# Two more head pairs of a windowed-attention kernel in the packed, split-operand form

## Chip, cores and metric

The kernel runs on one core of a Trainium2 chip. The metric is the device time of one execution in microseconds (us), lower is better. The three runs shown before the change have a median of 701.85 us (701.72 to 701.91).

## What is computed

Attention over a sliding window with a few sink keys, for 4 batches of 8 heads, 768 tokens and head size 64; then, on the 3072 rows of 512 numbers that the heads give together, a two-layer network with a leaky ReLU. All of it is float32, with the accuracy of float32.

```
scores = scale * q @ k.T
keep   = (pos[None, :] < n_sink) | ((rel >= 0) & (rel < window))   # n_sink = 4, window = 128
a      = softmax(where(keep, scores, -1e9))
x      = (a @ v).transpose(0, 2, 1, 3).reshape(B * S, H * D)
h      = x @ w_in                       # 512 -> 2048
out    = maximum(0.01 * h, h) @ w_out   # 2048 -> 512
```

## The kernel before

The work is cut into eight **units**: half a batch each, 384 tokens in T = 3 blocks of 128, even units the first half, odd ones the second. A unit has four **pairs** of heads. `attention_stream` does the attention of unit after unit, pair after pair, in small steps; `mlp_stream` does the two-layer network in 16 steps per unit (`fc` = 0 to 15, a slice of 128 of the 2048 hidden columns each). While the network works on unit u, the attention of unit u + 1 runs between its matmuls. TensorE's order is written out by this interleaving (TensorE is the one engine in `MANUAL`); the order on the other engines is the scheduler's, and each of them takes its instructions strictly in that order.

A step of the network: 12 matmuls into the bank `h` (line 554: three products of split operands for each of four column groups), then `g`: ScalarE's 0.01 h (564), VectorE's maximum (571), ScalarE's rounded copy `gh` (572), GpSimd's rest `gl` (573); and 9 matmuls of the second layer for the step before (591). In unit 0 every step writes the same bank `h`, so the matmuls of a step wait for VectorE's `g` of the step before.

Only while the network works on unit 0 are the weights made ready, two steps ahead: each step loads two slices (`wiraw`, `woraw`, line 173), VectorE turns the 64-bit numbers into float32 with three instructions for each slice (185, 187, 189), ScalarE rounds them (198) and GpSimd takes the rest (199). The raw slices go into the tag `raw` of `iopool`, which has three buffers.

A pair of heads has two forms, chosen by `native(u)`: units 0 and 1 are native, all others packed.

- **Native** (`attend`, first branch): one load `qkn` for two heads. For each block j two float32 matmuls with 64 rows each (299), a softmax of 260 columns for each head (311 on VectorE, 313 on ScalarE), and four float32 transposes (340) that ScalarE copies out (345). The sums go through two small VectorE instructions (323, 324), a broadcast on GpSimd (327) and transposes on TensorE (375, 378); VectorE applies them after the product with the values (407).
- **Packed** (second branch): one load `qkraw` for each head, with the operands twice. ScalarE rounds them (264) and GpSimd takes the two rests (265, 267): `split_head`. For each block two rounded matmuls with 128 rows (304); VectorE folds the 260 columns to 132 with a predicated copy (490) and a softmax over 132 (311). After three blocks VectorE scales the probabilities itself (497, 498, 499). `turn_packed` has three transposes (351) and, on VectorE, two masked products out of them (370), for the second head also the sink columns (356). `values` has one matmul for all sinks (391); VectorE takes the rest `xl` (412), and `split_sinks` another (257).

Packed heads load into the same tag `raw` as the weights, all but the first head of unit 2. `late_masks` builds the masks of the packed form in unit 1, pair 1.

Of the kernel before, what the change touches and what calls it, by code (L numbers as in the profile page):

```python
# [9 lines left out]
F32 = mybir.dt.float32  # L10
# [10 lines left out]
P = 128  # L21
B, H, S, D = 4, 8, 768, 64
DM, DF = 512, 2048
NB = S // P
NPAIR = H // 2
# [4 lines left out]
TU = T * P  # L30
NSK = 4
SKR = P
# [6 lines left out]
SCALE = 1.0 / D ** 0.5  # L39
MASKED = 1.0e38  # L40
DEEP = 9.0e8
NATU = 2
LEAD = 10
LEAD0 = 3
LAGT = 2
LAGG = 3
LAGV = 4
LAGP = 5
# [99 lines left out]
def fast_path(ctx, tc, cpool, qp, qk, vu, vs, vt, wq, out, ident, lims, wz, negm, wmin, wmax):  # L148
# [3 lines left out]
    xpool = ctx.enter_context(tc.tile_pool(name="xpool", bufs=2))  # L152
# [11 lines left out]
    raws, vraws, svs = {}, {}, {}  # L164
# [49 lines left out]

    def native(u):
        return u < NATU

    def load_pair(u, pair):  # L220
        b, half = divmod(u, 2)
        n = TU + NK[half]
        raw = apool.tile([P, TU + NK[1]], F32, tag="qksp", name=f"qkn{u}_{pair}")
        nc.sync.dma_start(out=raw[:, 0:n], in_=qp[half][pair])
        raws[u, pair] = raw

    def load_values(u, pair):
        b, half = divmod(u, 2)
        vr = apool.tile([P, 4 * P], F32, tag="v", name=f"v{u}_{pair}")
        nc.sync.dma_start(out=vr[:, 0:NVB[half] * P], in_=vu[half][b, pair])  # L230
        vraws[u, pair] = vr

    def load_head(u, h):
        b, half = divmod(u, 2)
        n = TU + NK[half]
        if native(u - 1) and h == 0:
            raw = apool.tile([P, TU + NK[1]], F32, tag="qksp", name=f"qkraw{u}_{h}")
        else:
            raw = iopool.tile([P, TU + NK[1]], F32, tag="raw", name=f"qkraw{u}_{h}", bufs=3)
        nc.sync.dma_start(out=raw[:, 0:n], in_=qk[half][b, h])  # L240
        raws[u, h] = raw

    def load_sinks(u, pair):
        if native(u):
            sv = apool.tile([SKR, TU], F32, tag="sv", name=f"sv{u}_{pair}")
            nc.sync.dma_start(out=sv[0:SKN, :], in_=vs[u // 2, pair])
            svs[u, pair] = sv
            return
        raw = xpool.tile([SKR, TU], F32, tag="rb", name=f"svr{u}_{pair}", bufs=1)[:, 0:P]
        nc.sync.dma_start(out=raw, in_=vt[u // 2, pair])  # L250
        svs[u, pair] = raw

# [30 lines left out]
    def score_bank(u, name):  # L283
        tags = ("s0", "s1", "o0", "o1") if u == 0 else ("s0", "s1")
        seq["s"] += 1
        return bank(tags[(seq["s"] - 1) % len(tags)], name)
# [6 lines left out]
    def scores(u, pair, j, heads, sp):  # L293
        k0, kn = KSL[u % 2][j]
        pss = [score_bank(u, f"s{u}_{2 * pair + o}_{j}") for o in heads]
        if native(u):
            for o, ps in zip(heads, pss):
                rows = slice(o * D, (o + 1) * D)
                nc.tensor.matmul(ps[:, 0:kn], lhsT=sp[rows, j * P:(j + 1) * P],  # L299
                                 rhs=sp[rows, TU + k0:TU + k0 + kn], start=True, stop=True)  # L300
        else:
            n = NK[u % 2]
            for c, off in enumerate((0, TU + n)):
                nc.tensor.matmul(pss[0][:, 0:kn], lhsT=sp[:, off + j * P:off + (j + 1) * P],  # L304
                                 rhs=sp[:, TU + k0:TU + k0 + kn], start=c == 0, stop=c == 1)
        return pss
# [8 lines left out]
    def segments(half):  # L315
        if half:
            return (0, 0, P), (P, 0, 2 * P), (3 * P, P, 2 * P), (5 * P, 2 * P, P)
        return (0, 0, 2 * P), (2 * P, P, 2 * P), (4 * P, 2 * P, P)
# [65 lines left out]

    def values(u, pair, state):
        half = u % 2
        acc = (turn_bank if native(u) else score_bank)(u, f"acc{u}_{pair}")
        vv, sv, st = vraws.pop((u, pair)), svs.pop((u, pair)), state["st"]
        packed, low = not native(u), P * (1 - half)
        if packed:  # L390
            nc.tensor.matmul(acc[:, low:TU], lhsT=sv, rhs=st[:, low:], start=True, stop=False, skip_group_check=True)  # L391
        parts = segments(half)
        for kb, (po, qo, m) in enumerate(parts):
            for o in range(2):
                nc.tensor.matmul(acc[o * D:(o + 1) * D, qo:qo + m],  # L395
                                 lhsT=vv[:, kb * P + o * D:kb * P + (o + 1) * D],
                                 rhs=state["pt"][:, o, po:po + m], start=kb == 0 and not packed,
                                 stop=packed and kb == len(parts) - 1, skip_group_check=True)
        for j in range(1 - half, 0 if packed else T):
            js = slice(j * P, (j + 1) * P)  # L400
            nc.tensor.matmul(acc[:, js], lhsT=sv[0:SKN, js], rhs=st, start=False, stop=j == T - 1,  # L401
                             skip_group_check=True)
        xh = xpool.tile([P, TU], F32R, tag=f"xh{pair}", name=f"xh{u}_{pair}")
        xl = xpool.tile([P, TU], F32R, tag=f"xl{pair}", name=f"xl{u}_{pair}")
        if native(u):
            xf = state["r"]
            nc.vector.tensor_tensor(out=xf, in0=acc[:, 0:TU], in1=xf, op=ALU.mult)
            (nc.gpsimd.tensor_copy if u == 0 and pair < NPAIR - 1 else nc.scalar.copy)(out=xh, in_=xf)
            nc.gpsimd.tensor_tensor(out=xl, in0=xf, in1=xh.bitcast(F32), op=ALU.subtract)
        else:  # L410
            nc.scalar.copy(out=xh, in_=acc[:, 0:TU])
            nc.vector.tensor_tensor(out=xl, in0=acc[:, 0:TU], in1=xh.bitcast(F32), op=ALU.subtract)
        xs[u].append((xh, xl))

    def ahead(u, pair):
        return (u, pair + 1) if pair < NPAIR - 1 else (u + 1, 0)
# [4 lines left out]
    def attend(u, pair, pend):  # L421
        state = {"sk": sks[pair % 2]}
        nxt = ahead(u, pair)

        def later(lag, f, join=False):
            pend.append((count[0] + lag, f, join))

        def fetch(o):
            more = nxt[0] < NU
            if native(u) and native(nxt[0]) and nxt not in raws:  # L430
                load_pair(*nxt)
            if more and o == 0:
                load_values(*nxt)
            if not native(u) and o == 0:
                load_head(u, 2 * pair + 1)
            elif more and not native(nxt[0]):
                load_head(nxt[0], 2 * nxt[1])

        def tile_pt():
# [4 lines left out]
            tile_pt()  # L444
            f(*args)

        if native(u):
            state["sm"] = apool.tile([P, T, 2], F32, tag="sm", name=f"sm{u}_{pair}")
            sp = raws.pop((u, pair))
            for j in range(T):  # L450
                kn = KSL[u % 2][j][1]
                pss = scores(u, pair, j, (0, 1), sp)
                w = apool.tile([P, 2, W3], F32, tag="pk", name=f"pk{u}_{pair}_{j}", bufs=3)
                a = P if kn == W3 else 0
                for o, ps in enumerate(pss):
                    soft(u, 2 * pair + o, j, w[:, o, 0:kn], ps[:, 0:kn], masks[min(T * (u % 2) + j, 2)],
                         state["sm"][:, j, o:o + 1])
                    nc.gpsimd.tensor_copy(out=state["sk"][:, 0, j, o, :], in_=w[:, o, a:a + NSK])
                if j == 0:
                    if waiting:  # L460
                        waiting.pop()(pss[1])
                    fetch(0)
                    if native(nxt[0]):
                        load_sinks(*nxt)
                    if u == 0 and pair == 0:
                        rest(anchor[0])
                    if u == 1 and pair == 1:
                        whole_lim.append(whole_limits(tc, cpool, lim_raw, lim_lo, anchor[0]))
                        late.append(late_masks(tc, cpool, iopool, masks, anchor[0]))
                count[0] += 1  # L470
                if j == T - 1:
                    if u == 0 and pair == 0:
                        waiting.append(lambda ps: spread(u, pair, state, ps))
                    else:
                        spread(u, pair, state, pss[1])
                later(LAGT, lambda j=j, w=w: pt_then(turn_native, u, pair, j, w, state))
                yield
        else:
            for o in range(2):
                h = 2 * pair + o  # L480
# [26 lines left out]
                        later(LAGT, lambda o=o, w=w: pt_then(turn_packed, u, pair, o, w, state))  # L507
                    yield
        last = u == 0 and pair == NPAIR - 1
        if native(u):  # L510
            later(LAGT if last else LAGG, lambda: gather(u, pair, state))
        later(LAGT if last else LAGV if native(u) else LAGP, lambda: values(u, pair, state), not native(u))

    def attention_stream():
        pend = []
# [121 lines left out]
    for x, _ in enumerate(mlp_stream()):  # L637
        u, r = divmod(x, mlp_steps)
# [216 lines left out]
```

## Time and profile before

| what | value |
|---|---|
| median of three runs | 701.85 us |
| the profiled execution | 701.92 us, its span 700.2 us |
| granted TensorE clock, mean | 0.997 |
| TensorE matmuls busy | 687.8 us (98%) |
| TensorE weight loads busy | 597.8 us (85%) |
| VectorE busy | 447.6 us (64%) |
| ScalarE busy | 318.3 us (45%) |
| GpSimd busy | 320.6 us (46%) |
| moved by DMA | 74.14 MB |

The shares are means over stages that differ: up to 35 us attention alone, up to 131 us unit 0 of the network with the weights made ready beside it, then units 1 to 7 without that work. A time in the trace counts from the start of the span. The span is the first to the last instruction; the execution's own time is 1.7 us longer.

### The profile page before, as it was taken

The page shows a single profiled execution, that of the slowest core. Times are in us where ns is not written, and L with a number is a line of the kernel's source. Part 1 is how long each engine was busy: PE and PEld are TensorE (multiplying, and loading weights), DVE is VectorE, ACT ScalarE, POOL GpSimd, SP SyncE. Part 2 cuts the span into 40 slices and gives each one's busy share as a digit, 9 for nine tenths or more (in the row PEclk, how much of TensorE's full clock was granted, in tenths as well). Part 3 has the DMA queues.
Part 4 walks back from the last instruction along what each step waited for, and adds up shares of the span by engine and source line. Part 5 has one row for each costly group of instructions (what it writes and reads, how often), then busy time and mean ns, then how long its engine had stood idle before and what let it go on. Part 6 is the DMA issues. An engine that isn't in the chain of part 4 may idle for free.

```text
span 700.2 us, 11523 instructions
## 1 busy us (share of the span) xinstructions
PE 687.8 (98%) x3950; PEld 597.8 (85%) x3950; DVE 447.6 (64%) x1183; ACT 318.3 (45%) x827; POOL 320.6 (46%) x442
## 2 busy tenths in 40 slices
PE   9999999999999999999999999999999999999996
PEld 5587788788888988888898888889888889889995
DVE  6798789655656665565566566556566565377772
ACT  5775566444444444444444444444444444222221
POOL 4676688544444543443454354354444444122220
PEclk9999999999999999999999999999999999999998
DMA  6655656412123112222122221121121220067741
GB/s 224 208 195 194 192 185 207 129 62 70 54 65 117 47 43 62 61 85 69 61 58 98 70 65 39 62 91 48 64 73 59 106 75 31 1 215 263 268 172 48
DMA packets 29535, 74.14 MB, mean 106 GB/s; under 512 B 3488, under 2 KB 9120, under 8 KB 29472
## 3 DMA queue, kind: packets, MB, share of 16 engines
q1 hardware_dynamic: 29184, 73.10, 31.3%
q8 instruction: 32, 0.52, 0.3%
q14 instruction: 31, 0.25, 0.1%
q10 hardware_dynamic: 288, 0.26, 0.1%
HBM read 67.06 MB, written 6.29 MB: 105 GB/s over the span
## 4 chain that ended last, share of the span: by engine, by line
PE 90%; DVE 4%; DMA 1%; ACT 1%; POOL 1%; issue 1%; SPq 0%; DVEq 0%; ACTq 0%; POOLq 0%
PE h L554 37%; PE o L591 36%; PE acc L395 5%; PE s L304 5%; PE t L351 3%; PE s L299 2%; PE t L340 1%; DMA qkn<-in_qp 1%; PE acc L401 1%; PE acc L391 0%; DMA qkraw<-in_qk 0%; ACT pk L313 0%; DVE pk L311 0%; PE t L353 0%; DVE ob L604 0%
## 5 line engine op out<-in xcount | busy, mean ns | idle before, releaser
L573 POOL TENSOR_TENSOR gl<-g,gh 128x384 fp32r<-128x384 f32 x127 | 129.9, 1023 | 276.3 <-ACT gh L572 259.0
L554 PE MATMUL h<-xh,wih 128*128 128x384 f32 x512 | 180.4, 352 | 1.6 <-DVE g L571 1.6
L554 PE MATMUL h<-xh,wil 128*128 128x384 f32 x512 | 172.7, 337 | 0.0
L554 PE MATMUL h<-xl,wih 128*128 128x384 f32 x512 | 172.6, 337 | 0.0
L591 PE MATMUL o<-woh,gh 128*128 128x512 f32 (+1 forms) x400 | 153.9, 386 | 0.2 <-DVE ob L604 0.2
L591 PE MATMUL o<-wol,gh 128*128 128x512 f32 (+1 forms) x400 | 153.1, 386 | 0.0
L313 ACT ACTIVATE pk<-pk,negm 128x132 f32<-128x132 f32 (+1 forms) x192 | 81.6, 426 | 92.3 <-DVE negm L311 92.1
L564 ACT ACTIVATE g<-h 128x384 f32<-128x384 f32 x127 | 62.0, 488 | 123.9 <-PE h L554 103.2
L591 PE MATMUL o<-woh,gl 128*128 128x512 f32 (+1 forms) x400 | 114.0, 387 | 0.0
L554 PEld LDWEIGHTS h<-xh,wih 128*128 128x128 f32 x512 | 96.3, 188 | 6.2 <-DVE g L571 2.8
L554 PEld LDWEIGHTS h<-xl,wih 128*128 128x128 f32 x512 | 96.7, 189 | 0.5
L572 ACT CAST gh<-g 128x384 fp32r<-128x384 f32 x128 | 65.7, 513 | 68.0 <-DVE g L571 67.8
L554 PEld LDWEIGHTS h<-xh,wil 128*128 128x128 f32 x512 | 96.1, 188 | 0.0
L571 DVE TENSOR_TENSOR g<-h,g 128x384 f32<-128x384 f32 x127 | 69.9, 550 | 30.2 <-ACT g L564 29.8
L591 PEld LDWEIGHTS o<-woh,gl 128*128 128x128 f32 x400 | 73.8, 188 | 16.9 <-POOL gl L573 0.5
L591 PEld LDWEIGHTS o<-woh,gh 128*128 128x128 f32 x400 | 75.1, 188 | 11.9 <-DVE ob L604 0.9
L591 PEld LDWEIGHTS o<-wol,gh 128*128 128x128 f32 x400 | 75.1, 188 | 11.5 <-issue 0.7
L490 DVE COPY_PREDICATED s<-tri,s 128x128 f32<-128x128 int8 x120 | 35.0, 292 | 53.0 <-PE s L304 50.9
L265 POOL TENSOR_TENSOR qksp<-qkraw,qksp 64x396 fp32r<-64x396 f32 (+1 forms) x48 | 56.4, 1176 | 20.4 <-POOL gl L573 19.1
L304 PEld LDWEIGHTS s<-qksp 128*128 128x128 f32 x288 | 53.5, 188 | 9.0 <-POOL qksp L267 0.5
L304 PE MATMUL s<-qksp 128*128 128x260 f32 (+1 forms) x288 | 56.5, 277 | 0.3 <-POOL qksp L267 0.3
L497 DVE TENSOR_SCALAR sm<-sm 128x3 f32<-128x3 f32 x48 | 37.6, 783 | 28.5 <-ACT pk L313 28.5
(114 smaller groups left out, 860.9 us busy)
## 6 DMA issues: line engine op xcount, KB each, us to landing
craw<-in_wq SPq DMA_DIRECT2D x32, 512.0 KB, 4.3
qkraw<-in_qk SPq DMA_DIRECT2D x24, 454.0 KB, 3.2
qkraw<-in_qk SPq DMA_DIRECT2D x24, 390.0 KB, 3.1
wiraw<-in_wq SPq DMA_DIRECT2D x16, 512.0 KB, 3.5
woraw<-in_wq SPq DMA_DIRECT2D x16, 512.0 KB, 3.3
out<-ob SPq DMA_DIRECT2D x23, 256.0 KB, 2.0
v<-in_vu SPq DMA_DIRECT2D x16, 256.0 KB, 2.6
v<-in_vu SPq DMA_DIRECT2D x16, 192.0 KB, 2.4
```

The source lines that it names most:

```text
L265: nc.gpsimd.tensor_tensor(out=sp[D:P, TU:TU + n], in0=raw[D:P, TU:TU + n], in1=sp[D:P, TU:TU + n].bitcast(F32), op=ALU.subtract)
L304: nc.tensor.matmul(pss[0][:, 0:kn], lhsT=sp[:, off + j * P:off + (j + 1) * P], rhs=sp[:, TU + k0:TU + k0 + kn], start=c == 0, stop=c == 1)
L313: nc.scalar.activation(out=w, in_=w, func=AF.Exp, scale=-1.0, bias=neg, accum_out=sm)
L395: nc.tensor.matmul(acc[o * D:(o + 1) * D, qo:qo + m], lhsT=vv[:, kb * P + o * D:kb * P + (o + 1) * D], rhs=state["pt"][:, o, po:po + m], s ...
L490: nc.vector.copy_predicated(out=ps[:, W1:W3], mask=late[0][1], data=ps[:, 0:P])
L497: nc.vector.tensor_scalar(out=sm, in0=sm, scalar1=1e-9, scalar2=None, op0=ALU.add)
L554: nc.tensor.matmul(ph[:, 0:TU], lhsT=w[:, cs], rhs=x, start=cc == 0 and c == 0, stop=cc == NCC - 1 and c == 2)
L564: nc.scalar.mul(g, ph[:, 0:TU], 0.01)
L571: anchor[0] = nc.vector.tensor_tensor(out=g, in0=ph[:, 0:TU], in1=g, op=ALU.max)
L572: nc.scalar.copy(out=gh, in_=g)
L573: (nc.vector if step == NU * NFC - 1 else nc.gpsimd).tensor_tensor(out=gl, in0=g, in1=gh.bitcast(F32), op=ALU.subtract)
L591: nc.tensor.matmul(acc, lhsT=(gl if c == 2 else gh)[:, t * P:(t + 1) * P], rhs=(wl if c == 1 else wh)[:, cols], start=f == 0 and c == 0, s ...
```

## The change

The form is chosen pair by pair. Pairs 0 to 5 stay native, so pairs 2 and 3 of unit 1 take the packed form. The load that has a buffer of its own is now that of the first packed head, wherever it lies, and the first packed pair's sink values go into a buffer of the tag `r`.

```diff
-NATU = 2
+NATP = 6
...
-    def native(u):
-        return u < NATU
+    def native(u, pair):
+        return u * NPAIR + pair < NATP
...
-        if native(u - 1) and h == 0:
+        if u * H + h == 2 * NATP:
             raw = apool.tile([P, TU + NK[1]], F32, tag="qksp", name=f"qkraw{u}_{h}")
...
-        raw = xpool.tile([SKR, TU], F32, tag="rb", name=f"svr{u}_{pair}", bufs=1)[:, 0:P]
+        if u * NPAIR + pair == NATP:
+            raw = xpool.tile([SKR, P + TU], F32, tag="r", name=f"svr{u}_{pair}")[:, 0:P]
+        else:
+            raw = xpool.tile([SKR, TU], F32, tag="rb", name=f"svr{u}_{pair}", bufs=1)[:, 0:P]
```

All other lines of the diff pass `pair` on. The lines behind stand 3 or 4 numbers later.

VectorE, unit 0 of the network, the stretch that ends with `g` of step 9 (`di`/`do` and `wi`/`wo` are the weights, `pk_3` the softmax tiles of the native pair 3). Before:

```order
L311 ISA pk_3_1_1246,negm<-s_6_1_1242,m_96 128x260
L311 ISA negm 128x1
L189 SCALAR_TENSOR_TENSOR wo_1125<-woraw_1118,do_1126 128x512
L311 ISA pk_3_1_1246,negm<-s_7_1_1243,m_96 128x260
L311 ISA negm 128x1
L185 TENSOR_SCALAR di_1196<-wiraw_1191 128x512
L187 SCALAR_TENSOR_TENSOR di_1196<-wiraw_1191,di_1196 128x512
L189 SCALAR_TENSOR_TENSOR wi_1195<-wiraw_1191,di_1196 128x512
L185 TENSOR_SCALAR do_1201<-woraw_1193 128x512
L311 ISA pk_3_2_1311,negm<-s_6_2_1307,m_96 128x260
L311 ISA negm 128x1
L571 TENSOR_TENSOR g_9_1292<-h_9_1273,g_9_1292 128x384
```

Here are three softmaxes between the weights. The same place in the changed kernel (`pk_5` and `pk_6` are heads 5 and 6, packed):

```order
L187 SCALAR_TENSOR_TENSOR di_1185<-wiraw_1180,di_1185 128x512
L500 TENSOR_SCALAR sm_5_1099<-sm_5_1099 128x3
L314 ISA pk_6_1277,negm<-s_6_0_1279,pm_675 128x132
L314 ISA negm 128x1
L189 SCALAR_TENSOR_TENSOR wi_1184<-wiraw_1180,di_1185 128x512
L501 RECIPROCAL sm_5_1099<-sm_5_1099 128x3
L493 COPY_PREDICATED s_6_1_1309<-tri,s_6_1_1309 128x128
L185 TENSOR_SCALAR do_1190<-woraw_1182 128x512
L502 TENSOR_TENSOR pk_5_1098<-pk_5_1098,sm_5_1099 128x396
L314 ISA pk_6_1277,negm<-s_6_1_1309,pm_675 128x132
L314 ISA negm 128x1
L575 TENSOR_TENSOR g_9_1294<-h_9_1263,g_9_1294 128x384
```

The scaling of one head and the softmax of the next now stand between the instructions of one weight slice.

VectorE again, the end of the weights: the last slice is `wo` of step 15. In the changed kernel it stands ahead of `g` of step 13:

```order
L359 TENSOR_TENSOR st_3_1601<-t_3_1_1596,own 128x384
L187 SCALAR_TENSOR_TENSOR do_1585<-woraw_1577,do_1585 128x512
L373 TENSOR_TENSOR pt_3_1474<-t_3_1_1596,low 128x3x128
L373 TENSOR_TENSOR pt_3_1474<-t_3_1_1596,upp 128x3x128
L189 SCALAR_TENSOR_TENSOR wo_1584<-woraw_1577,do_1585 128x512
L493 COPY_PREDICATED s_0_2_1626<-tri,s_0_2_1626 128x128
L575 TENSOR_TENSOR g_13_1611<-h_13_1589,g_13_1611 128x384
```

Before, it stood ahead of `g` of step 14:

```order
L257 TENSOR_TENSOR sv_1_1833<-svr_1_1737,sv_1_1833 32x128
L490 COPY_PREDICATED s_1_1_1662<-tri,s_1_1_1662 128x128
L189 SCALAR_TENSOR_TENSOR wo_1570<-woraw_1563,do_1571 128x512
L311 ISA pk_1_1619,negm<-s_1_1_1662,pm_674 128x132
L311 ISA negm 128x1
L571 TENSOR_TENSOR g_14_1671<-h_14_1652,g_14_1671 128x384
```

Up to `g` of step 14 both orders hold the same instructions otherwise, except that `xl` of pair 3 and one of the four `sv` rests now stand behind it.

## Rows read from the trace of the kernel before

**Rows 1.** The page's chain of waits, shares of the span by engine.
```profile
PE 90%; DVE 4%; DMA 1%; ACT 1%; POOL 1%; issue 1%; SPq 0%; DVEq 0%; ACTq 0%; POOLq 0%
```
**Rows 2.** Busy time by stage: window, its length, each engine's busy us (instructions), clock, DMA.
```profile
53.00:124.00 71.00, 70.35 (x411) 57.18 (x410) 60.68 (x127) 42.14 (x99) 52.93 (x60) 1.00 0.57 195
...
220.00:300.00 80.00, 80.00 (x465) 70.67 (x464) 47.47 (x131) 35.96 (x95) 34.90 (x47) 1.00 0.19 57
```
**Rows 3.** VectorE's waits between 53 and 124 us: total us, times, longest.
```profile
DVE r L407 <- PE acc L401: 2.8, 2, 1.5
DVE pk L311 <- PE t L340: 2.7, 3, 1.6
DVE g L571 <- ACT g L564: 1.6, 3, 0.7
DVE pk L311 <- PE s L299: 0.6, 2, 0.4
```
**Rows 4.** The chain in order of time: start us, us, what; values of native, then packed pairs.
```profile
56.29 1.45 PE acc L395 x16
...
76.67 1.45 PE acc L395 x16
...
104.30 2.08 PE o L591 x9
106.62 1.56 PE h L554 x9
...
223.88 1.45 PE acc L395 x16
...
244.62 1.45 PE acc L395 x16
```
**Rows 5.** VectorE's timeline, a native pair: start us, us, instruction.
```profile
81.55 0.43 DVE L311 CUSTOM_DVE_ANT_0 pk<-s,m 128x260 f32<-128x260 f32 x1 [0.68 <-PE t L340]
...
82.25 0.69 DVE L185 TENSOR_SCALAR di<-wiraw 128x512 int32<-128x512 int32 x1
...
99.64 0.55 DVE L407 TENSOR_TENSOR r<-acc,r 128x384 f32<-128x384 f32 x1
```
**Rows 6.** Busy time of a window in unit 3, one packed pair and four steps.
```profile
224.00:244.50 20.50, 20.50 (x120) 18.21 (x118) 12.95 (x35) 9.36 (x24) 9.57 (x12) 1.00 0.19 56
```
**Rows 7.** VectorE's and GpSimd's groups by line: count, busy us, mean ns, idle before.
```profile
L571 DVE TENSOR_TENSOR g<-h,g 128x384 f32<-128x384 f32 x127 | 69.9, 550 | 30.2 <-ACT g L564 29.8
...
L257 DVE TENSOR_TENSOR sv<-svr,sv 32x128 fp32r<-32x128 f32 x24 | 7.9, 330 | 31.1 <-ACT sv L256 31.1
...
L265 POOL TENSOR_TENSOR qksp<-qkraw,qksp 64x524 fp32r<-64x524 f32 x24 | 31.6, 1315 | 10.7 <-POOL gl L573 10.7
```
**Rows 8.** The instructions on the tile `sm`: duration ns min/median/max, first and last start.
```profile
L497 DVE TENSOR_SCALAR sm<-sm x48: 157/768/1055, 114.1 to 600.8; 128x3 f32<-128x3 f32 x48
...
L499 DVE TENSOR_TENSOR pk<-pk,sm x48: 558/1180/1253, 116.6 to 601.3; 128x396 f32<-128x396 f32 x48
L323 DVE TENSOR_SCALAR s<-sm x8: 159/162/168, 10.7 to 93.5; 128x6 f32<-128x6 f32 x8
```
**Rows 9.** VectorE's timeline: two idle places, `g` of step 14, a third idle place.
```profile
58.64 0.56 DVE L407 TENSOR_TENSOR r<-acc,r 128x384 f32<-128x384 f32 x1 [1.30 <-PE acc L401]
60.84 0.43 DVE L311 CUSTOM_DVE_ANT_0 pk<-s,m 128x260 f32<-128x260 f32 x1 [1.63 <-PE t L340]
...
124.00 0.55 DVE L571 TENSOR_TENSOR g<-h,g 128x384 f32<-128x384 f32 x1
...
125.52 0.43 DVE L370 TENSOR_TENSOR pt<-t,low 128x256 f32<-128x256 f32 x1 [0.97 <-ACT pt L365]
```
**Rows 10.** The timelines of GpSimd and VectorE, unit 2's first packed head beside the weights.
```profile
113.41 1.29 POOL L199 TENSOR_TENSOR wil<-wi,wih 128x512 fp32r<-128x512 f32 x1 [0.38 <-ACT wih L198]
...
114.14 0.59 DVE L497 TENSOR_SCALAR sm<-sm 128x3 f32<-128x3 f32 x1
```
**Rows 11.** Loads issued between 60 and 150 us: KB each, median us to landing.
```profile
qkraw<-in_qk SPq DMA_DIRECT2D x8, 390.0 KB, 3.4
```

More of the change, by code (lines that the diff above doesn't have):

```diff
@@ L243, in load_sinks @@
     def load_sinks(u, pair):
-        if native(u):
+        if native(u, pair):
             sv = apool.tile([SKR, TU], F32, tag="sv", name=f"sv{u}_{pair}")
@@ L295, in scores @@
         pss = [score_bank(u, f"s{u}_{2 * pair + o}_{j}") for o in heads]
-        if native(u):
+        if native(u, pair):
             for o, ps in zip(heads, pss):
@@ L386, in values @@
         half = u % 2
-        acc = (turn_bank if native(u) else score_bank)(u, f"acc{u}_{pair}")
+        acc = (turn_bank if native(u, pair) else score_bank)(u, f"acc{u}_{pair}")
         vv, sv, st = vraws.pop((u, pair)), svs.pop((u, pair)), state["st"]
-        packed, low = not native(u), P * (1 - half)
+        packed, low = not native(u, pair), P * (1 - half)
         if packed:
@@ L404, in values @@
         xl = xpool.tile([P, TU], F32R, tag=f"xl{pair}", name=f"xl{u}_{pair}")
-        if native(u):
+        if native(u, pair):
             xf = state["r"]
@@ L429, in fetch @@
             more = nxt[0] < NU
-            if native(u) and native(nxt[0]) and nxt not in raws:
+            if native(u, pair) and native(*nxt) and nxt not in raws:
                 load_pair(*nxt)
@@ L433, in fetch @@
                 load_values(*nxt)
-            if not native(u) and o == 0:
+            if not native(u, pair) and o == 0:
                 load_head(u, 2 * pair + 1)
-            elif more and not native(nxt[0]):
+            elif more and not native(*nxt):
                 load_head(nxt[0], 2 * nxt[1])
@@ L445, in pt_then @@
             f(*args)
-        if native(u):
+        if native(u, pair):
             state["sm"] = apool.tile([P, T, 2], F32, tag="sm", name=f"sm{u}_{pair}")
@@ L462, in attend @@
                     fetch(0)
-                    if native(nxt[0]):
+                    if native(*nxt):
                         load_sinks(*nxt)
@@ L509, in attend @@
         last = u == 0 and pair == NPAIR - 1
-        if native(u):
+        if native(u, pair):
             later(LAGT if last else LAGG, lambda: gather(u, pair, state))
-        later(LAGT if last else LAGV if native(u) else LAGP, lambda: values(u, pair, state), not native(u))
+        later(LAGT if last else LAGV if native(u, pair) else LAGP, lambda: values(u, pair, state),
+              not native(u, pair))
     def attention_stream():
```

## Prediction

> **What bounds the kernel now.** I read the chain of waits first, because it says which engine the end hangs on: TensorE carries nine tenths of it, VectorE 4% [rows 1]. A reader could stop there and conclude that TensorE time taken out is time won. So I next asked for busy time by stage. The pairs that change run between the network's steps on unit 0: the first of their scores stand at 53 us, and the last `g` that the weights press on, that of step 14, starts at 124.00 us [rows 9]. In that stage of 71 us TensorE is busy for 70.35 us, but VectorE for 60.68 us, 85% [rows 2]. Later, from 220 to 300 us, TensorE is just as full while VectorE is down to 47.47 of 80 us, 59% [rows 2]. The difference is the weights. So the changed pairs lie in the one long stretch where two engines are nearly full at once, and what counts is how much room VectorE has. Its waits in the stage, taken together, are 2.8 + 2.7 + 1.6 + 0.6 = 7.7 us [rows 3]; the remaining 2.6 us are gaps too small to be listed, of the kind that stands between dependent instructions.
>
> **What the change does on TensorE.** Two native pairs go, two packed pairs come. I price them by the distance of the values of one pair from those of the next. In unit 1 that is 76.67 - 56.29 = 20.38 us [rows 4]. Between those two places TensorE's order has 69 matmuls of the network, of 21 in a step. Nine of the second layer take 2.08 us and nine of the first 1.56 us [rows 4], twelve of them then 2.08 us, so a step is 4.16 us and 69 matmuls are 13.7 us. A native pair thus holds TensorE for 6.7 us. In unit 3 the distance is 244.62 - 223.88 = 20.74 us [rows 4] with 84 matmuls, 16.6 us, between: a packed pair is 4.1 us. That is 2.6 us less for each pair, 5.2 us for both, if nothing else is late.
>
> **What it does on VectorE.** A native pair has three blocks of two softmaxes, 82.25 - 81.55 = 0.70 us a block [rows 5], the product at the end, 0.55 us [rows 5], and two small ones, the sum's 0.16 us [rows 8] and a reciprocal that I set as long: 2.10 + 0.55 + 0.32 = 3.0 us. A packed pair has six predicated copies, six softmaxes, two scalings of three instructions, four masked products, the sink product, `xl` and the `sv` rest. A window of unit 3 holds one such pair and four steps: 12.95 us of VectorE [rows 6], of which four `g` of 0.55 us [rows 7] are 2.2 us. The pair is 10.75 us. That is measured where VectorE has pauses; where it has none, an instruction starts before the tail of the last one is over (two softmaxes of 0.43 us start 0.35 us apart, since both fit in the 0.70 us [rows 5]). With 0.08 us less on some nine short ones I take 10.0 us. A packed pair costs VectorE 7.0 us more than a native one, two cost 14.0 us.
>
> Not all of that is due before `g` of step 14: the order puts one `xl` (as long as a `g`, 0.55 us) and one `sv` rest (0.33 us [rows 7]) behind it, 0.9 us, and behind it VectorE stands idle for 0.97 us at once [rows 9], which takes them. So 13.1 us come into the stage. What hides them is idle VectorE time, 7.7 us, but not all of that: the two idle places at 58.64 and 60.84 us, 1.30 + 1.63 us [rows 9], lie ahead of the first packed head's softmax, which still waits there for the same values and transposes of the pairs before. 4.8 us can be filled. **The sum: 13.1 - 4.8 = 8.3 us by which `g` of step 14 comes later.** In this unit the next matmuls into the bank `h` wait for `g`, and TensorE is full from there on, so nothing gives it back. The 5.2 us that TensorE no longer needs are spent waiting. Against the profiled execution, 701.92 us, this makes **710.2 us**; that execution is 0.07 us above the median of the runs shown, which I neglect.
>
> **The other edits.** GpSimd gets the splits of four heads, two subtractions each, the longer one 1.32 us [rows 7], so at most 8 x 1.32 = 10.6 us, less the native pairs' own; it has 71 - 52.93 = 18 us of room [rows 2]. If that room were gone, `gl` would be late and TensorE would wait at the second layer. ScalarE is busy for 42.14 of 71 us [rows 2] and I count it at nothing. SP's queue gets two loads where it had one for each pair, and three of the four new ones share the three `raw` buffers with the weights; the DMA engines are at 0.57 [rows 2], and steps stretched by VectorE leave more time for each landing. I count them at nothing too; the price if this cover fails is a rival below.
>
> **Bounds of the price.** The instructions that swing most are the scaling ones: 157 to 1055 ns with a median of 768 for the first, 558 to 1253 with 1180 for the third [rows 8]. If all four heads got the shortest, a pair would cost 10.0 - 2 x (0.61 + 0.62) = 7.5 us, the two 9.0 us more than native, and if every idle us were filled too: 9.0 - 0.9 - 7.7 = +0.4 us, 702.3 us. If they got the longest, 10.7 us a pair, and no idle us could be filled: 15.4 - 0.9 = +14.5 us, 716.4 us. I stay at the median, because these instructions now stand beside weight work on GpSimd, as the first packed head of unit 2 does already. There the first of them, alone 0.16 us, starts at 114.14 us and ends at 114.73 us, while GpSimd's weight subtraction runs from 113.41 to 114.70 us [rows 10]: it ended when GpSimd ended.
>
> The Trainium skill, "SBUF — State Buffer", section "Who interferes with whom", has the rule for that: VectorE and GpSimd share one pair of ports under an exclusive lock, and a VectorE instruction in a two-port mode, or with two SBUF inputs, blocks fully behind a GpSimd instruction that reads SBUF. The trace agrees at that place. As an estimate, were all eight scaling instructions to wait out a whole subtraction of 1.29 us, each would be some 0.67 us above its median, and the sum would be 8.3 + 5.4 us, 715.6 us, instead of 710.2 us.
>
> **The rivals.**
> *TensorE still decides, and the change is faster.* The chain gives nine tenths to TensorE [rows 1], and the changed order has the last weights a step earlier, ahead of `g` of step 13, so a VectorE that finds the scaling short and its pauses fillable might keep up. Then the 5.2 us are won: 696.7 us. It decides from the point where the two pairs cost VectorE less than the room in the stage, 7.7 us less the 5.2 us by which the stage would shrink: 2.5 us, against 14.0 us as priced. That is far off, but the price comes from another unit. Chance 0.15.
> *The gaps and the lead of the weights take all of it.* The weights are made two steps ahead; a VectorE late with them costs nothing until that lead is used up, if `g` itself is served in time. The order works against it, since `g` stands in the same queue behind the added instructions. No change, about 701.9 us. Chance 0.12.
> *The loads.* A head's load holds one of three `raw` buffers until its split, and SP's queue stands still behind a load without a buffer, so a weight slice comes late by up to a landing, 3.4 us [rows 11]. For four heads that is 13.6 us; half of it beside VectorE's own lateness makes 8.3 + 6.8 = 15.1 us, 717.0 us. Against it: with VectorE the slower part the buffers have time. Chance 0.08.
>
> **How the numbers follow.** The forecast keeps 0.65, between 702.3 and 716.4 us. A measurement of this kernel can tell about 0.2%, 1.4 us, from no change. Faster is the first rival, 0.15. Same is the second, 0.12, which also stands for the lowest end of the forecast. Slower is the forecast and the loads, 0.73. The range leaves out the first rival and the tails: 701.5 to 717.0 us.
>
> **What would show it.** Right: VectorE busy for over 90% of the stage between 53 us and `g` of step 14; that `g` near 132 us; TensorE with several us of waits there that end on `g` (line 575) or on what VectorE gives it; the four new scalings as long as the old ones; from unit 1 on both traces the same but shifted. Wrong: TensorE full through the stage and `g` of step 14 before 124 us (the first rival); VectorE idle while it waits for a weight load (the loads); or a VectorE price of the packed pair far from 10 us, seen in the durations of the lines 493, 314, 500 to 502, 373, 359 and 415.

## The result, and the profile after

The changed kernel takes 711.90 us (median of 4 runs, 711.19 to 712.78) against 701.79 us for the kernel before beside it (4 runs, 699.60 to 701.91): a ratio of 1.0144, 95% interval 1.0130 to 1.0158. The forecast was 710.2 us. The profiled execution took 712.14 us, its span 710.3 us, 10.1 us more than before.

The page of the changed kernel, its table of busy times, its strip of TensorE's clock and its chain by engine:

```profile
PE 686.9 (97%) x3922; PEld 598.8 (84%) x3922; DVE 457.3 (64%) x1215; ACT 316.8 (45%) x825; POOL 328.1 (46%) x442
...
PEclk9999998999999999999999999999999999999999
...
PE 84%; DVE 7%; POOL 3%; DMA 2%; issue 2%; ACT 1%; SPq 0%; DVEq 0%; ACTq 0%; POOLq 0%
```

TensorE executes 28 matmuls fewer than before, yet it was busy for 0.9 us less only (687.8 before). It gave 6% of the chain away, half of it to VectorE, most of the rest to GpSimd and the DMAs [rows 1]. Busy time by stage (window, its length, then busy us of TensorE, its weight loads, VectorE, ScalarE and GpSimd with instructions in brackets, granted clock, DMA share, GB/s):

```profile
53.00:124.00 71.00, 58.47 (x324) 48.89 (x324) 63.12 (x141) 36.24 (x85) 55.32 (x57) 0.95 0.59 201
53.00:131.84 78.84, 66.31 (x359) 56.04 (x359) 69.63 (x159) 39.92 (x95) 60.49 (x63) 0.94 0.58 194
90.00:100.00 10.00, 5.36 (x27) 4.08 (x26) 9.15 (x22) 4.36 (x10) 7.04 (x8) 0.97 0.45 151
100.00:110.00 10.00, 10.00 (x56) 8.33 (x56) 8.88 (x20) 5.10 (x13) 8.56 (x10) 0.86 0.66 230
110.00:120.00 10.00, 6.33 (x32) 4.74 (x30) 9.65 (x24) 4.72 (x13) 6.48 (x6) 1.00 0.58 194
120.00:124.00 4.00, 1.05 (x4) 1.06 (x5) 2.53 (x4) 1.06 (x2) 3.89 (x6) 0.50 0.79 274
124.00:135.00 11.00, 11.00 (x62) 9.37 (x61) 8.54 (x22) 5.47 (x15) 6.28 (x8) 0.88 0.31 93
220.00:300.00 80.00, 80.00 (x465) 70.83 (x465) 49.94 (x138) 35.66 (x93) 35.82 (x47) 1.00 0.21 67
```

The first line answers to the first of [rows 2]: TensorE loses 11.9 us of busy time in the same 71 us. Of these, 10.7 us lie in three places: 90 to 100, 110 to 120 and 120 to 124 us, where it was busy for 9.72, 10.00 and 3.73 us before. The last line shows the later stage as it was. The second line is the stretch up to `g` of step 14, which VectorE's timeline now has at 131.84 us where it had 124.00 [rows 9]:

```profile
131.84 0.56 DVE L575 TENSOR_TENSOR g<-h,g 128x384 f32<-128x384 f32 x1 [0.46 <-ACT g L568]
```

So this `g` comes 7.84 us later; 8.3 us were forecast. The idle time in its brackets says more: VectorE was standing still and waited for ScalarE's 0.01 h, the first thing made from the bank `h`, so TensorE was the late one at that place. Nor is 7.84 us the delay that lasts. TensorE's first matmul behind this `g` into the bank `h`, that of step 15, before and now, and the values of pair 3, now:

```profile
124.61 0.45 PE L554 MATMUL h<-xh,wih 128*128 128x384 f32 x1 [0.88 <-DVE g L571]
```
```profile
132.44 1.52 PE L398 MATMUL acc<-pt,v 128*64 128x128 f32 x16
...
134.98 0.34 PE L558 MATMUL h<-xh,wih 128*128 128x384 f32 x1
```

Step 15 starts 10.37 us later and no longer waits for `g`. In the kernel before, the values of pair 3 stood ahead of `g` of step 14 (at 116.40 us); now they stand behind it, so that this `g` had less of TensorE's work ahead of it than before.

TensorE's waits between 40 and 150 us (engine, line, what it waited for: us in total, times, longest) were 1.9 us in all before:

```profile
PE h L554 <- DVE g L571: 1.6, 2, 0.9
PE s L304 <- POOL qksp L267: 0.3, 1, 0.3
```

Now:

```profile
PE t L356 <- POOL sk L508: 5.2, 2, 4.2
PE s L307 <- POOL qksp L268: 3.2, 2, 2.9
PE h L558 <- DVE g L575: 1.6, 3, 0.8
PE s L307 <- POOL qksp L270: 1.4, 2, 0.7
PE s L307 <- DVE xl L415: 1.2, 1, 1.2
PE t L354 <- DVE pk L502: 0.7, 1, 0.7
```

That is 13.3 us, 11.4 more than before, and 9.8 us of it end on GpSimd: on the sink columns of a packed head (line 508) and on its split operands (268, 270). Only 3.5 us end on VectorE.

From unit 2 on everything is shifted: its first sink matmul (394, before 391) starts at 152.09 us where it started at 141.72, 10.37 us later, and in unit 3 the value matmuls start at 234.16 instead of 223.81 us. So the loss closes as a sum: 11.4 us more waits, 0.9 us less busy time, 10.5 us; measured 10.37. I use this sum for the experiments below as well; there it agrees with the shift at unit 2 within 1.1 us.

### The two long waits

The chain of waits in order of time (start us, us, what) shows where the wait for head 7's operands, the one of 2.93 us in TensorE's timeline, comes from:

```profile
91.89 0.70 DVE wo L189
92.61 3.38 DMA qkraw<-in_qk
96.01 0.95 ACT qksp L267
```
```profile
98.44 0.39 PE L307 MATMUL s<-qksp 128*128 128x260 f32 x1 [2.93 <-POOL qksp L268]
```

The head's load, for which SP's queue had waited 3.0 us, was issued at the moment when VectorE finished a weight slice and thereby gave a `raw` buffer back. VectorE's lateness thus reaches TensorE without a single wait on VectorE: by a buffer, a load, ScalarE's rounding and GpSimd's rest.

The other one, GpSimd's timeline around 120 us (start us, us, instruction):

```profile
117.83 1.23 POOL L268 TENSOR_TENSOR qksp<-qkraw,qksp 64x396 fp32r<-64x396 f32 x1
119.14 0.99 POOL L270 TENSOR_TENSOR qksp<-qkraw,qksp 128x384 fp32r<-128x384 f32 x1
120.09 1.27 POOL L199 TENSOR_TENSOR wil<-wi,wih 128x512 fp32r<-128x512 f32 x1
121.30 0.20 POOL L505 CAST sk<-pk 128x24 fp32r<-128x24 f32 x1
121.45 1.27 POOL L199 TENSOR_TENSOR wol<-wo,woh 128x512 fp32r<-128x512 f32 x1
122.68 0.21 POOL L508 TENSOR_TENSOR sk<-pk,sk 128x12 f32<-128x12 f32 x1
```

VectorE's scaling of that head started at 117.48 us and lasted 0.69 us. The two small sink instructions that need it take 0.41 us together, but in the order of GpSimd's queue they stand behind the splits of a later head (the second of unit 2) and behind two weight slices, one of them between the two; TensorE stands still for 4.17 us, until 122.95.

### TensorE's clock

The granted clock, 1.00 in the whole stage before [rows 2], is now 0.86 behind the first long wait, and 0.50 in and 0.88 behind the second, in the windows above. TensorE's timeline after the second (start us, us, instruction):

```profile
122.95 0.48 PE L356 MATMUL t<-ident,sk 128*128 128x128 f32 x1 [4.17 <-POOL sk L508]
...
125.58 0.63 PE L595 MATMUL o<-woh,gh 128*128 128x512 f32 x1
126.00 0.63 PE L595 MATMUL o<-wol,gh 128*128 128x512 f32 x1
...
127.04 0.39 PE L595 MATMUL o<-woh,gh 128*128 128x512 f32 x1
127.27 0.39 PE L595 MATMUL o<-wol,gh 128*128 128x512 f32 x1
```

Matmuls of one shape start 0.42 us apart, then 0.23 us: the lower level of 1.2 GHz, then 2.4 GHz again.

### The profile page after: what moved, and what is told of

It is laid out like the page before. It is cut to its first block, busy times and chain, and to the rows that moved or that the text cites. A ratio compares the mean times of both kernels' runs of the same rounds, so it can differ in the third digit from the quotient of the medians.

```text
span 710.3 us, 11519 instructions
## 1 busy us (share of the span) xinstructions
PE 686.9 (97%) x3922; PEld 598.8 (84%) x3922; DVE 457.3 (64%) x1215; ACT 316.8 (45%) x825; POOL 328.1 (46%) x442
## 4 chain that ended last, share of the span: by engine, by line
PE 84%; DVE 7%; POOL 3%; DMA 2%; issue 2%; ACT 1%; SPq 0%; DVEq 0%; ACTq 0%; POOLq 0%
PE h L558 34%; PE o L595 34%; PE acc L398 5%; PE s L307 5%; PE t L354 3%; PE s L302 1%; POOL wol L199 1%; PE t L343 1%; DVE do L185 1%; POOL wil L199 1%; DVE do L187 1%; DVE wo L189 1%; DVE di L187 1%; DVE di L185 1%; DVE pk L314 1%
## 5 line engine op out<-in xcount | busy, mean ns | idle before, releaser
L268 POOL TENSOR_TENSOR qksp<-qkraw,qksp 64x524 fp32r<-64x524 f32 (+1 forms) x52 | 61.9, 1190 | 29.1 <-POOL gl L577 19.6
L493 DVE COPY_PREDICATED s<-tri,s 128x128 f32<-128x128 int8 x132 | 38.4, 291 | 54.7 <-PE s L307 52.7
L307 PEld LDWEIGHTS s<-qksp 128*128 128x128 f32 x312 | 58.2, 189 | 16.2 <-POOL qksp L268 4.1
L307 PE MATMUL s<-qksp 128*128 128x260 f32 (+1 forms) x312 | 62.4, 280 | 5.8 <-POOL qksp L268 3.2
L267 ACT CAST qksp<-qkraw 128x908 fp32r<-128x908 f32 (+1 forms) x52 | 47.0, 904 | 27.4 <-PE s L307 23.5
```

The source lines that it names most:

```text
L267: nc.scalar.copy(out=sp[:, 0:TU + n], in_=raw[:, 0:TU + n])
L268: nc.gpsimd.tensor_tensor(out=sp[D:P, TU:TU + n], in0=raw[D:P, TU:TU + n], in1=sp[D:P, TU:TU + n].bitcast(F32), op=ALU.subtract)
L493: nc.vector.copy_predicated(out=ps[:, W1:W3], mask=late[0][1], data=ps[:, 0:P])
```

## Experiments

Three theories. **V**: VectorE's queue is the cause, as forecast. **G**: GpSimd's queue, with more to do for packed heads, holds TensorE. **L**: the heads' loads, which share the `raw` buffers with the weights, come late. The table has all runs; "waits" is the sum of TensorE's listed waits between 40 and 150 us, "busy" that of its matmuls over the span, "unit 2" the start of its first sink matmul. Each ratio is to the runs of the kernel before on the same chip. The order on every engine but TensorE is the scheduler's, so an edit below can also move instructions that it does not touch (a_scale_act has an example); no run here parts such a move from the work itself.

| kernel | us | ratio to before, 95% | waits | busy | unit 2 |
|---|---|---|---|---|---|
| before | 701.79 | 1 | 1.9 | 687.8 | 141.72 |
| the change | 711.90 | 1.0144 (1.0130 to 1.0158) | 13.3 | 686.9 | 152.09 |
| d_dve | 710.78 | 1.0113 (1.0085 to 1.0142) | 6.2 | 692.3 | 151.12 |
| d_pool | 704.46 | 1.0038 (1.0024 to 1.0053) | 5.2 | 687.5 | 144.60 |
| d_ring | 703.34 | 1.0021 (1.0005 to 1.0037) | 3.6 | 687.6 | 144.09 |
| a_natp7 | 705.12 | 1.0038 (1.0024 to 1.0053) | 5.9 | 687.1 | 145.15 |
| a_scale_act | 705.02 | 1.0036 (1.0022 to 1.0049) | 8.5 | 683.5 | 144.69 |
| a_sk_dve | 709.35 | 1.0110 (1.0080 to 1.0140) | 10.0 | 686.7 | 149.32 |
| b_light | 700.34 | 0.9971 (0.9940 to 1.0002) | 0.7 | 686.9 | 140.71 |
| a_light | 706.59 | 1.0061 (1.0040 to 1.0082) | 8.8 | 685.2 | 146.05 |
| a_nosplit | 706.94 | 1.0061 (1.0042 to 1.0079) | 8.6 | 685.6 | 146.46 |
| a_light_nosplit | 702.48 | 1.0006 (0.9990 to 1.0022) | 6.5 | 683.4 | 142.58 |
| a_scale_nosplit | 704.20 | 1.0026 (1.0015 to 1.0038) | 7.3 | 684.1 | 143.91 |
| c_natp7_scale | 704.21 | 1.0035 (1.0019 to 1.0051) | 3.9 | 687.4 | 144.18 |

### One load at a time on the kernel before

Two copies for each softmax of unit 1's pairs 2 and 3, on VectorE alone:

```diff
+                    if u == 1 and pair >= 2:
+                        for _ in range(2):
+                            nc.vector.tensor_copy(out=ps[:, 264:512], in_=ps[:, 0:248])
```

> The kernel before, all native, with 24 extra copies of 248 columns on VectorE (within the score banks), two behind each softmax of pairs 2 and 3 of unit 1: some 24 x 0.35 = 8.4 us of VectorE work, about what the changed kernel adds there (8.95 us by its trace), and nothing on GpSimd, the loads or TensorE. Theory V (VectorE's queue is what fills up): 5 to 9 us slower than before, 707 to 711 us. Theory G (GpSimd's queue) and theory L (loads that share the raw buffers with the weights): under 2 us slower, below 704 us.

Busy time up to `g` of step 14, which starts at 131.91 us in this run:

```profile
53.00:131.91 78.91, 74.58 (x411) 60.31 (x410) 67.09 (x155) 44.17 (x101) 50.79 (x59) 0.96 0.55 177
```

V holds as a sufficient cause. VectorE is busy for 67.09 us instead of the 60.68 us of [rows 2], 6.4 us more, and that `g` comes 7.91 us later. The sum by TensorE reads otherwise than in the change: 4.3 us more waits, and 4.5 us more busy time for the same 3950 matmuls. The clock is 0.96 over these 78.91 us, which is 3.2 us of full speed: over a third of the loss of 9.4 us at unit 2 is TensorE at its lower level.

The same for GpSimd, 20 subtractions, and for the buffers, four more head loads that each hold a `raw` buffer for half a pair:

```diff
...
+                if u == 1 and pair >= 2 and j in (0, 2):
+                    for _ in range(5):
+                        nc.gpsimd.tensor_tensor(out=junk, in0=sp[:, 0:192], in1=sp[:, 192:384], op=ALU.subtract)
```

> The kernel before, all native, with 20 extra subtractions of 192 columns on GpSimd in pairs 2 and 3 of unit 1, five for each head: some 20 x 0.5 = 10 us, about the splits of four packed heads. Nothing is added on VectorE or to the loads. Theory G: 4 us slower or more, above 706 us. Theories V and L: under 2 us slower, below 704 us.

```diff
...
+                if u == 1 and pair >= 2 and j in (0, 2):
+                    held.append(hold(2 * pair + j // 2))
...
```

> The kernel before, all native, with four extra loads of a packed head's 454 KB into the raw buffers of the weights, issued in pairs 2 and 3 of unit 1, each held for about half a pair and let go by a one-column copy on ScalarE. Theory L: 3 us slower or more, above 705 us. Theories V and G: under 1.5 us slower, below 703.5 us.

Ratios of 1.0038 and 1.0021: neither work alone makes the loss, though neither is free. d_ring comes out against L; d_pool lies between the two expectations, and it is a weak test of G. Its subtractions, on which nothing waits, started between 39.0 and 81.1 us, where the change has its long waits on GpSimd between 91 and 123 us.

### One pair instead of two

```diff
-NATP = 6
+NATP = 7
```

> The changed kernel with only the last pair of unit 1 packed (NATP = 7). Theory V: the room on VectorE is used first and half the work is added, so less than half of the 10 us: 2 to 5 us slower than before, 704 to 707 us. Theory L or G, by which each packed pair brings its own waits: half, about 5 us, 707 us. If TensorE's saving counted for a single pair: 699 us.

The last pair alone costs a third of what both cost (unit 2 comes 3.43 us later, against 10.37), as V expected. By this the cost grows faster than the number of pairs; pair 2 alone was not run.

### Parts of the change taken off VectorE or GpSimd

ScalarE scales the probabilities of unit 1's packed heads:

```diff
-                        nc.vector.tensor_tensor(out=w, in0=w, in1=sm.rearrange("p (j o) -> p j o", o=1)
-                                                .broadcast_to([P, T, W1]), op=ALU.mult)
+                        if u == 1:
+                            for i in range(T):
+                                nc.scalar.activation(out=w[:, i], in_=w[:, i], func=AF.Copy, scale=sm[:, i:i + 1])
+                        else:
...
```

> The changed kernel; for the packed heads of unit 1 ScalarE scales the probabilities (three instructions of 132 columns for each head) in place of VectorE's one of 396. VectorE has 4 x 1.1 = 4.3 us less, ScalarE some 12 x 0.4 = 5 us more, of which it has room. Theory V: 3 to 5 us faster than the changed kernel, 707 to 709 us. Theories G and L: within 1.5 us of it, 710.5 to 712.5 us.

More than V expected: 7.4 us of the 10.37 are gone at unit 2, for four instructions of VectorE that took 1.52, 0.56, 1.20 and 0.69 us in the change, 4.0 us together. TensorE's waits between 40 and 150 us in this run:

```profile
PE s L307 <- POOL qksp L268: 2.6, 2, 2.3
PE h L562 <- POOL wil L199: 1.7, 2, 1.2
...
PE t L356 <- POOL sk L512: 0.2, 1, 0.2
```

The sink wait is nearly gone (5.2 to 0.2 us); waits fall by 4.8 us in all, since a weight slice (199) takes some of it. Part of this can be the order: on GpSimd the two sink instructions of head 7 now follow each other, at 114.08 and 114.36 us, ahead of the splits behind which they stood in the change (now at 116.43 us). The granted clock is 1.00 in every window of the stage, and TensorE's busy time falls by another 3.4 us, from 686.9 to 683.5. As the matmuls are the same 3922 in both, I put those 3.4 us down to the lower clock in the change. Against the kernel before TensorE is now busy for 4.3 us less: this is the change's saving, known to about 1 us (b_light below has the matmuls of the kernel before and 0.9 us less).

Is it then GpSimd's sinks that cost? They go to VectorE:

```diff
-                        nc.gpsimd.tensor_copy(out=sk[:, 0:3:2, 0:T, o, :].bitcast(F32R),
+                        eng = nc.vector if u == 1 else nc.gpsimd
+                        eng.tensor_copy(out=sk[:, 0:3:2, 0:T, o, :].bitcast(F32R),
...
```

> The changed kernel; for the packed heads of unit 1 VectorE makes the rounded sinks and their rest (two small instructions for each head) in place of GpSimd, where TensorE waited for them for 5.2 us in all behind head splits and weight rests. VectorE gets 8 x 0.2 = 1.6 us more. Theory G (TensorE waits because of GpSimd's queue): 3 to 5 us faster than the changed kernel, 707 to 709 us. Theory V (the wait is only where a lateness from VectorE comes out): no faster, 711 to 714 us.

Two to three us better, between the two expectations. TensorE waits for the same columns, now 3.7 us on VectorE. So most of the loss does not hang on GpSimd being the one that makes them.

### VectorE relieved by much, and the heads' splits left out

If V were all, 15 us of room on VectorE should bring the saving to light. The second instruction of each weight slice is left out from slice 5 on, in the change and, as its fair comparison, in the kernel before:

```diff
-            nc.vector.scalar_tensor_tensor(out=d, in0=top, scalar=-0x40000000, in1=d,
-                                           op0=ALU.bitwise_and, op1=ALU.bitwise_or)
+            if fc < 5:
+                nc.vector.scalar_tensor_tensor(out=d, in0=top, scalar=-0x40000000, in1=d,
+                                               op0=ALU.bitwise_and, op1=ALU.bitwise_or)
```

> The changed kernel without the second of the three instructions that turn a weight slice into float32 for steps 5 to 15 (the sign and top bit of those weights are left out): 22 x 0.7 = 15 us less on VectorE in the stage, nothing else. Theory V: with that room TensorE's saving comes out; 3 to 5 us faster than the all-native kernel with the same left out, so 695 to 698 us where that one has 700 to 701 us. Theories G and L: the packed pairs still cost, so it stays 2 us or more slower than that one.

> The kernel before with the same left out: the second of three weight instructions for steps 5 to 15. All theories: TensorE is full there already, so only the 1.6 us of its waits for VectorE can go: 700 to 701.5 us. It is the base for the changed kernel with the same left out.

V alone falls here: 706.59 against 700.34 us, unit 2 still 5.34 us later. The room was less than 15 us: over the span VectorE's busy time fell from 457.3 to 446.4 us in the change, and from 447.6 to 432.2 in the kernel before. But with 446.4 us VectorE has no more to do than in the kernel before, where TensorE waited for 1.9 us. ScalarE's waits between 48 and 145 us in the lightened change name what is late next:

```profile
ACT qksp L268 <- DMA qkraw<-in_qk: 7.0, 3, 3.2
```

ScalarE waited for three head loads, 7.0 us in all. So the splits went next. Heads 5 to 7 take the split tile of head 4:

```diff
     def load_head(u, h):
+        if u == 1 and h > 4:
+            return
...
-                sp = split_head(u, h)
+                sp = split_head(u, h) if u != 1 or h == 4 else kept[0]
+                kept[:] = [sp]
```

> Heads 5 to 7 of unit 1 take the split tile of head 4 again, so that three loads through the raw buffers, three ScalarE roundings and six GpSimd subtractions are left out (the output differs there); VectorE's work stays as in the changed kernel. Theory V (VectorE's queue alone): the time stays within 2 us of the changed kernel's 711.9, 709.9 or more. Theory L or G (loads and GpSimd's queue carry part): 704 to 708, and TensorE's waits on the split tile are gone.

> As the run before, and also without the second weight instruction for slices 5 to 15, some 15 us less on VectorE (the output differs). The fair comparison is the kernel before with the same left out, 700.3. If VectorE and the head's loads and splits together are the whole cost, TensorE's saving of 5.2 us shows: 695 to 699. If VectorE alone was the cause, the same as with the splits, 706.6. If scaling and sinks still hold TensorE: 702 to 705.

> The changed kernel with ScalarE scaling the probabilities of unit 1's packed heads, and heads 5 to 7 taking the split tile of head 4 (the output differs). With the splits the scaling on ScalarE gave 705.0. V: without the splits still 704 or more, since VectorE's work is the same. L or G: 698 to 702, below the kernel before.

a_nosplit comes out as L and G said: 5 us less than the change with VectorE's instructions untouched, though 2.3 of the 4.6 us of waits on split tiles remain. It leaves out loads, roundings and splits together, so it does not part L from G. a_scale_nosplit comes out as V said: once the scaling is off VectorE, leaving the splits out gains 0.8 us. The gains do not add: 7.4 and 5.6 us at unit 2 one by one, 8.2 us together. With both VectorE's weights and the splits relieved 1.87 us remain against b_light (unit 2 at 142.58 against 140.71), and the 4.3 us still do not show: 702.48 us lie in the last of the three ranges expected. TensorE's waits there:

```profile
PE t L361 <- POOL sk L514: 3.0, 1, 3.0
PE h L564 <- DVE g L581: 2.0, 3, 0.9
```

6.5 us of waits against 0.7, 3.5 us less busy: a sum of 2.3 us. It is the sink columns once more, which come at the end of a head's whole chain.

### The candidate

One pair, its scaling on ScalarE (the two diffs above together):

> Only the last pair of unit 1 packed, with ScalarE scaling its probabilities: the candidate to come level with the kernel before. One packed pair alone gave 705.1, 3.3 above before; the scaling on ScalarE gave back 7 of 10 us for two pairs. V: 3.3 less half of 7, within 1.4 of the kernel before, 700.4 to 703.2. L or G: the load and the GpSimd part of one head pair stay, 703 to 705.

704.21 us, as L or G said; V missed, and against one pair without this edit (705.12) the gain is 0.9 us. The ratio is 1.0035, its interval above 1: no version here that does all of the work beats the kernel before, or comes level with it. A fourth `raw` buffer, which would part the heads' loads from the weights, wasn't tried.

## Why the prediction came out right, point by point

**The direction and the size** were right: 711.9 us against 710.2, in the range. The place was right as well: the stage of the weights, and behind it a plain shift. The size is in part luck, as the next points show.

**VectorE's price, 13.1 us, was too high.** Its busy time up to `g` of step 14 grew from 60.68 to 69.63 us, by 8.95 us. VectorE's groups between 53 and 132 us name part of the difference (count | busy us, mean ns | idle before):

```profile
L502 DVE TENSOR_TENSOR pk<-pk,sm 128x396 f32<-128x396 f32 x5 | 5.4, 1075 | 0.0
...
L500 DVE TENSOR_SCALAR sm<-sm 128x3 f32<-128x3 f32 x5 | 2.8, 561 | 1.5 <-ACT pk L316 1.5
...
L373 DVE TENSOR_TENSOR pt<-t,upp 128x384 f32<-128x384 f32 x4 | 2.2, 547 | 0.0
...
L415 DVE TENSOR_TENSOR xl<-acc,xh 128x384 fp32r<-128x384 f32 x1 | 0.5, 547 | 0.0
```

The masked products and `xl` last 0.55 us, as the trace of before has them in unit 3, but the two scaling instructions were taken at their medians, 1180 and 768 ns [rows 8]. The groups of five hold one of unit 2; the four of unit 1 took 3.97 and 2.32 us instead of 4.72 and 3.07 us, 1.5 us less. For the rest I have an estimate only. The overlap that I took for nine short instructions of a pair also holds for long ones: `xl` of 0.55 us starts at 111.64 us and the next instruction at 112.11, 0.08 us before its end. For the other 16 of a pair's 25 that is 1.3 us, 2.6 us for both pairs. Together 4.1 of the 4.15 us. Where VectorE has room the forecast's price does show: over the span it is busy for 14.2 us more in a_light than in b_light (446.4 against 432.2 us), and the two pairs had been priced at 14.0 us.

**The idle time that was to be filled, 4.8 us, was not.** VectorE's time without work was 71 - 60.68 = 10.3 us and is 78.84 - 69.63 = 9.2 us: 1.1 us were filled. Old waits went and others came, among them 2.6 us on weight loads, which did not stand in [rows 3] and were the prediction's sign for the rival of the loads (VectorE's waits between 53 and 134 us):

```profile
DVE r L410 <- PE acc L404: 1.6, 1, 1.6
...
DVE do L185 <- DMA woraw<-in_wq: 1.5, 2, 1.3
...
DVE di L185 <- DMA wiraw<-in_wq: 1.1, 2, 0.8
```

So 8.95 - 1.1 = 7.84 us stands beside a forecast of 13.1 - 4.8 = 8.3: the two terms were each off by about 4 us, in opposite directions. That the sum came close is luck, and so is the place where it was taken: the `g` of step 13 came 11.42 us later (126.94 against 115.52), that of step 14 7.84 us and that of step 15 10.36 us (140.04 against 129.68).

**"VectorE busy for over 90%"** was not quite so: 69.63 of 78.84 us, 88%. **"TensorE's waits end on `g` or on what VectorE gives it"** was wrong as read from the list: 3.5 of 13.3 us. Behind the other waits VectorE stands partly, through the `raw` buffer at 92.6 us for one; d_dve shows that its lateness alone suffices, and in a_scale_act most of the loss goes with 4.0 us of its work.

**"The other edits at nothing"** is the step that failed. GpSimd had its 18 us of room, as counted, and yet TensorE's waits ended on it for 9.8 us: 5.2 us on sink columns, whose 0.4 us of work stood behind nearly 5 us of others in GpSimd's order, and 4.6 us on splits. And loads and splits were not free: without those of three heads the time falls by 5 us (a_nosplit). The rival of the loads had part of the mechanism, not as an addition but as a way by which VectorE's lateness travels: with the scaling off VectorE the same leaving out gains 0.8 us.

**TensorE's saving, 5.2 us, was 4.3 us**, and it was spent waiting, as forecast. It did not show even in a_light_nosplit, with 22 weight instructions off VectorE and three heads' splits gone. Which of the queues of a packed head's chain would have to be changed for it to show stays open.

**"The next matmuls into the bank `h` wait for `g`"** failed at the very place: in the change they start 2.6 us behind `g` of step 14 (131.84 + 0.56 us, then 134.98). **"TensorE is full from there on"** is right. Between that `g` and the first sink matmul of unit 2 the two traces read (window, length, then as above):

```profile
124.00:141.72 17.72, 16.38 (x88) 14.81 (x89) 11.59 (x36) 8.81 (x26) 10.33 (x13) 1.00 0.39 127
```
```profile
131.84:152.09 20.25, 19.41 (x115) 16.89 (x113) 13.11 (x36) 9.12 (x27) 9.17 (x13) 1.00 0.28 92
```

The change takes 2.5 us longer there, which is the difference of 10.37 and 7.84 us. It is neither waits nor clock: TensorE stands idle for 0.8 instead of 1.3 us, at 1.00, and executes 27 matmuls more, those that the order moved behind this `g`. The forecast took `xl` and an `sv` rest off for that, but not the matmuls ahead of them. It had no term for the clock either, which costs about 3.4 us of TensorE's busy time in the stage.

**The scaling beside GpSimd** goes as at the place in [rows 10]. The scaling at 73.57 us lasts 1.52 us, beside a weight subtraction that starts 0.21 us earlier and lasts 1.30 us:

```profile
73.57 1.52 DVE L502 TENSOR_TENSOR pk<-pk,sm 128x396 f32<-128x396 f32 x1
```
```profile
73.36 1.30 POOL L199 TENSOR_TENSOR wol<-wo,woh 128x512 fp32r<-128x512 f32 x1 [1.86 <-ACT woh L198]
74.62 1.34 POOL L577 TENSOR_TENSOR gl<-g,gh 128x384 fp32r<-128x384 f32 x1
```

It ends at 75.09 us, 0.43 us after the subtraction, and the `gl` that GpSimd starts meanwhile lasts 1.34 us instead of the 1.03 us of its mean over the span. The Trainium skill, "SBUF — State Buffer", section "Who interferes with whom", says that a VectorE instruction with two SBUF inputs and a GpSimd instruction that reads SBUF exclude each other, and that the order of issue decides which one waits. Both directions agree with these rows. The time worked out by that rule alone, 715.6 us, did not come: the scaling at 117.48 us, beside no weight subtraction, took 0.69 us, and the mean of the five is 1.075.

## What to carry to other kernels

When an edit turns one engine's work into short requests to all the others, price the way of one item through their queues, not only each engine's busy time: TensorE waited 4.2 us for 0.4 us of work on an engine with a quarter of its time free. A shared buffer ring carries lateness between engines that have no dependence on each other. And where single reliefs of 7 and 6 us give 8 together, the waits cover each other, so an experiment that removes one of them says what is gained with the others still in place, not what it costs by itself.

## What was not expected of the hardware

TensorE's granted clock fell from 1.00 to 0.86 in the ten us behind a wait of 2.93 us, and to 0.50 and then 0.88 in and behind one of 4.17 us; matmuls of 128x512 started 0.42 instead of 0.23 us apart until it rose. In a_scale_act, which has 8.5 us of waits in the stage but none over 2.3 us, it stayed at 1.00. In d_dve, whose longest listed wait is 1.5 us, it fell in two places, to 0.89 between 70 and 80 us and to 0.83 between 100 and 110 us, and TensorE was busy for 4.5 us more with the same 3950 matmuls. In c_natp7_scale, whose longest is 1.0 us, it was 0.98 between 53 and 140 us. Thus the length of the longest wait alone does not say when it falls; what else does, these runs do not show.
